# Second net of a three-stage kernel put under the planner that orders the first two stages

## The chip, the core and the metric

One core of one Trainium2 chip runs the whole program. The metric is the device time of one execution in microseconds. Three runs of the kernel before took 1053.13, 1054.54 and 1055.58 us (median 1054.54). The execution that was profiled took 1055.07 us, of which the trace spans 1053.2 us from the first to the last instruction. Engines are named as in the profile: PE (TensorE, with PEld for its weight loads), DVE (VectorE), ACT (ScalarE), POOL (GpSimd) and SP (SyncE, which here only issues DMAs).

## The reference, cut to what matters

```python
# 1. retention: q, k, v of 4 batches, 8 heads, 768 positions, 64 features
state = gamma * state + einsum('bhd,bhe->bhde', k[:, :, t], v[:, :, t])
y[:, :, t] = scale * einsum('bhd,bhde->bhe', q[:, :, t], state)
x = y as (3072 tokens, 512)
# 2. first net: w_in (512, 2048), w_out (2048, 512)
h = x @ w_in
g = where(h >= 1, h, where(h <= -1, 0, (h + 1)**2 / 4))
x = g @ w_out
# 3. second net: w1, w2 (512, 1024), w3 (1024, 1024), w_out (1024, 512)
out = ((x @ w1) * (x @ w2)) @ w3 @ w_out
```

All arrays are float32.

## The kernel before

**Arithmetic.** Every product of the two nets is made of three matmuls of 128x128 by 128x512 in the type fp32r: an operand is split into a high half (ACT casts it to fp32r) and a low half (DVE subtracts the high half from the source), and high·high, low·high and high·low are summed in one PSUM bank. So nearly each operand costs one ACT and one DVE instruction, a "split", before PE can use it.

**The second net.** Its two last weights are multiplied first: 16 units of 12 matmuls (8 for each half of w3) give w3·w_out in four PSUM banks a half, and each bank is split into a tile `wc`. Units read w3's rows from DRAM, where an earlier stage left them (`w3f`), and split them (`w3s`). The 6 token tiles are then taken as 3 pairs. For a pair, 14 operands (`yop`) are split from the first net's output and its sums and differences; for each of 8 blocks f of 128 hidden features a weight "unit" is loaded (`unit_w`), split, summed and split again, and 7 products p1, p2, p6, p5, p7, p3, p4 of 6 matmuls each go to the banks a, c and b. This gives both tiles' a and b by 7 products where 8 would be needed directly. ACT and DVE join them to the two gated products `c`, which are split into `p` and `q`. The products of `p` with `wc` (L984, banks `oacc`) stand between the products of the next block; those of `q` follow at the pair's end, 24 matmuls for each of 4 token groups t. `oacc` has 4 banks; each finished bank is copied out (`ost`, on DVE for even t, on ACT for odd t) and stored.

**What sets the order.** Stages 1 and 2 are recorded as operations of a planner (class `Plan`): each has an engine, a cost, the values it reads and writes, and slots of named pools ("tags") that its values need. `set_due` walks back from PE's list, which is written out by hand, and gives each operation a due time; `emit` then issues, at every step, the operation that could start first, among those of an engine the one due soonest, and PE may take any ready one of its next 12. What `emit` issues on an engine stays in that order on the chip: each engine runs its own list in order and waits at an instruction until its semaphores are there. The second net is not in that plan: it is emitted after `plan.emit` (L1174) by the loops of L1195 to L1254, in the order in which they are written. There `load_w3(u + 1)` stands ahead of `emit_w3o(u)` (L1196, L1197), the unit's sums are GpSimd's (L904), and at a pair's end the next pair's splits are written between the blocks and the copies of `oacc`:

```python
            for x in out_blocks(NF2 - 2):
                emit_out(*x)
            if more:
                while ahead[0][1] == 0:
                    split_y(*ahead.pop(0))
                fetch_y1(i + 1, 1, range(4))
            for x in out_blocks(NF2 - 1):
                emit_out(*x)
                evac_out(2 * i, x[3], x[0])
```

The tiles of w3's split halves come from a pool of two on the right side of SBUF (`late[1]`, tag "ws", L862), made once the weight conversion's pool is closed (L1176). The first net's operands `g` and `wo` use a pool of ten slots, tag "wo" (L285). A weight that arrives as 64-bit words is converted by `convert` (two ACT and four DVE instructions a KB row); seven of w3's eight row blocks are converted before and spilled to DRAM, one (`DIRECT`) at the end of the first net.

## Time and profile before

| | us |
|---|---|
| median of 3 runs | 1054.54 (1053.13 to 1055.58) |
| the profiled execution | 1055.07 |
| its span in the trace | 1053.2 |
| from the first to the last start of PE in the second net | 618.26 to 1048.94 |

The first two stages fill the span up to about 617 us, w3·w_out runs to 668 us, and the three pairs follow at 668, 799 and 928 us or so. A timeline row gives the start and the duration in us; an idle time in brackets stands ahead of the row's first instruction, with the engine and line that ended it. Matmul durations overlap (they are pipelined), so the pace of PE is read from start to start.

### The profile page before, as it was taken

Reading aid. Unit: us, or ns where it says so; the run is one execution under the profiler, and the core shown is the slowest. Engines: PE = TensorE matmul, PEld = TensorE weight load, DVE = VectorE, ACT = ScalarE, POOL = GpSimd, SP = SyncE. Lnnn points to the kernel's source line nnn. Section 1 sums busy time; section 2 is a strip of 40 time slices with the busy share of each in tenths; the row PEclk is TensorE's granted clock in tenths of the full one; section 3 lists DMA queues with packets and bytes.
Section 4 is the critical chain, followed back from the end, with each engine's and each line's share of the span. In section 5 each row is a group of like instructions: output and inputs, shape, how many; then the busy total and the mean of one; then the engine's idle time right before and its main releaser. Section 6 shows DMA issues by size and latency. Waiting matters only on the chain.

```text
span 1053.2 us, 14552 instructions
## 1 busy us (share of the span) xinstructions
PE 1020.0 (97%) x5444; PEld 824.1 (78%) x5444; DVE 644.6 (61%) x957; ACT 500.8 (48%) x845; POOL 165.5 (16%) x221
## 2 busy tenths in 40 slices
PE   8899999999999999999999989899989999899998
PEld 5778878877877788888887868688867888678886
DVE  6887479734465684777776657465573556635550
ACT  2477457533344552566666535444442444334330
POOL 1212332222232100000000000222211322022210
PEclk8999999999999999999999999899999999899999
DMA  9997959757979689781453963112122120221102
GB/s 291 239 308 239 317 182 407 286 193 275 372 256 381 201 309 338 262 295 65 180 179 101 347 231 101 40 41 84 37 90 91 40 80 21 101 80 41 40 1 80
DMA packets 71051, 190.18 MB, mean 181 GB/s; under 512 B 8898, under 2 KB 9282, under 8 KB 69060
## 3 DMA queue, kind: packets, MB, share of 16 engines
q1 hardware_dynamic: 63104, 163.34, 45.7%
q0 software_dynamic: 7584, 25.70, 6.3%
q8 instruction: 43, 0.70, 0.3%
q14 instruction: 28, 0.23, 0.1%
q10 hardware_dynamic: 292, 0.20, 0.1%
HBM read 139.40 MB, written 49.81 MB: 180 GB/s over the span
## 4 chain that ended last, share of the span: by engine, by line
PE 85%; DMA 6%; ACT 3%; DVE 2%; SPq 1%; issue 1%; POOL 0%; DVEq 0%; POOLq 0%; ACTq 0%
PE bank_a L946 12%; PE y1acc L277 8%; PE y1acc L279 8%; PE y1acc L278 8%; PE bank_b L946 6%; PE hps L277 5%; PE hps L279 5%; PE hps L278 5%; PE oacc L987 4%; PE oacc L989 4%; PE oacc L988 4%; PE bank L731 4%; PE banks L731 3%; PE bank_c L946 3%; DMA raw<-in_w_in_dram 3%; PE pa L530 1%
## 5 line engine op out<-in xcount | busy, mean ns | idle before, releaser
L904 POOL TENSOR_TENSOR unit_w<-unit_w 128x256 f32<-128x256 f32 x96 | 70.9, 738 | 576.4 <-DVE unit L274 570.8
L277 PE MATMUL y1acc<-g,wo 128*128 128x512 f32 x384 | 151.7, 395 | 2.4 <-DMA wo<-wo_d 1.3
L946 PE MATMUL bank_a<-yop,unit 128*128 128x512 f32 x576 | 147.6, 393 | 6.3 <-ACT c L961 4.3
L279 PE MATMUL y1acc<-g,wo 128*128 128x512 f32 x384 | 149.8, 390 | 0.0
L278 PE MATMUL y1acc<-g,wo 128*128 128x512 f32 x384 | 149.6, 390 | 0.0
L946 PEld LDWEIGHTS bank_a<-yop,unit 128*128 128x128 f32 x576 | 108.4, 189 | 30.2 <-ACT c L961 4.7
L277 PE MATMUL hps<-xh,win 128*128 128x512 f32 x256 | 102.9, 402 | 2.9 <-ACT xh L573 1.8
L279 PE MATMUL hps<-xl,win 128*128 128x512 f32 x256 | 100.6, 393 | 0.0
L278 PE MATMUL hps<-xh,win 128*128 128x512 f32 x256 | 100.6, 393 | 0.0
L277 PEld LDWEIGHTS y1acc<-g,wo 128*128 128x128 f32 x384 | 72.1, 188 | 20.8 <-ACT r L613 1.7
L973 DVE TENSOR_TENSOR c<-bank_b,c 128x512 f32<-128x512 f32 x24 | 16.6, 692 | 115.6 <-PE bank_b L946 115.6
L613 ACT ACTIVATE r<-hps 128x512 f32<-128x512 f32 x64 | 38.2, 597 | 98.8 <-PE hps L279 97.3
L279 PEld LDWEIGHTS y1acc<-g,wo 128*128 128x128 f32 x384 | 72.1, 188 | 15.5 <-DVE g L338 0.4
L278 PEld LDWEIGHTS y1acc<-g,wo 128*128 128x128 f32 x384 | 72.1, 188 | 14.5
L336 ACT CAST g<-g 128x512 fp32r<-128x512 f32 x80 | 48.9, 620 | 68.1 <-PE y1acc L279 59.0
L616 DVE SCALAR_TENSOR_TENSOR r<-hps,r 128x512 f32<-128x512 f32 x64 | 44.0, 688 | 53.5 <-ACT r L615 52.9
L946 PE MATMUL bank_b<-yop,unit 128*128 128x512 f32 x288 | 74.0, 393 | 0.0
L338 DVE TENSOR_TENSOR g<-g 128x512 fp32r<-128x512 f32 x64 | 44.8, 713 | 32.9 <-ACT g L336 32.8
L946 PEld LDWEIGHTS bank_b<-yop,unit 128*128 128x128 f32 x288 | 54.8, 190 | 11.7
L274 DVE TENSOR_TENSOR unit<-unit_w,unit 128x512 fp32r<-128x512 f32 x96 | 57.2, 617 | 8.2 <-ACT unit L273 8.2
L277 PEld LDWEIGHTS hps<-xh,win 128*128 128x128 f32 x256 | 48.6, 190 | 16.8 <-DVE r L616 3.0
L621 POOL DMA_DIRECT2D g_d<-r x64 | 37.3, 583 | 138.1 <-DVE r L616 130.2
(186 smaller groups left out, 1935.8 us busy)
## 6 DMA issues: line engine op xcount, KB each, us to landing
wo<-wo_d SPq DMA_DIRECT2D x64, 512.0 KB, 5.5
g_d<-r POOLq DMA_DIRECT2D x64, 256.0 KB, 5.0
g<-g_d SPq DMA_DIRECT2D x64, 256.0 KB, 5.3
unit_w<-sp_wab SPq DMA_DIRECT2D x24, 512.0 KB, 3.5
wo_d<-wo POOLq DMA_DIRECT2D x16, 512.0 KB, 7.3
raw<-in_w_dram SPq DMA_DIRECT2D x16, 512.0 KB, 6.8
raw<-in_w3t_dram SPq DMA_DIRECT2D x8, 1024.0 KB, 7.6
raw<-in_w_in_dram SPq DMA_DIRECT2D x28, 256.0 KB, 7.9
```

Source lines behind the costliest of these rows:

```text
L274: nc.vector.tensor_tensor(out=lo, in0=src, in1=hi, op=ALU.subtract)
L277: nc.tensor.matmul(out=ps, lhsT=lh, rhs=rh, start=first, stop=False)
L278: nc.tensor.matmul(out=ps, lhsT=ll, rhs=rh, start=False, stop=False)
L279: nc.tensor.matmul(out=ps, lhsT=lh, rhs=rl, start=False, stop=last)
L336: plan.op("ACT", 0.63, lambda: nc.scalar.copy(out=dst.ap[:, 0, :], in_=at()), r=[src], w=[dst, hi], bound=bound)
L338: return plan.op("DVE", 0.7, lambda: nc.vector.tensor_tensor(out=dst.ap[:, 1, :], in0=at(), in1=dst.ap[:, 0, :], op=ALU.subtract), r=[src, ...
L616: plan.op("DVE", 0.7, lambda: nc.vector.scalar_tensor_tensor(out=r.ap, in0=ps.ap, scalar=1.0, in1=r.ap, op0=ALU.max, op1=ALU.min), r=[ps], ...
L731: nc.tensor.matmul(out=at[where](), lhsT=l, rhs=r, start=first and kb + k == 0, stop=kb == 1 and k == 2, skip_group_check=True,)
L904: nc.gpsimd.tensor_tensor(out=block(u, o), in0=block(u, x), in1=block(u, y), op=op)
L946: nc.tensor.matmul(out=ps, lhsT=x, rhs=z, start=first and kb + k == 0, stop=kb == 1 and k == 2, skip_group_check=True,)
L987: nc.tensor.matmul(out=ps, lhsT=lh, rhs=wh, start=(f == 0), stop=False)
L988: nc.tensor.matmul(out=ps, lhsT=lh, rhs=wl, start=False, stop=False)
```

## The change

The second net's operations are recorded with `plan.op` too, before the one call of `emit`; their PE operations are appended to PE's list by hand, in nearly the order that the loops had, and the planner chooses where ACT, DVE, SP put theirs. The unit's sums become DVE operations, because the second net now uses the first net's `plan_unit`. The split halves of w3 take slots of the tag "wo". Stores are marked `store`: they are due 6 us after what they store, and are not counted among the loads that hold SP's window of 30 us. `DIRECT` falls to 0 and `FEW` rises to 4, so that all eight blocks of w3 are spilled, and the last conversions are due 14 us ahead instead of 4. Two pools are closed and others opened by operations of the plan (`close_conversion`, and `close_pairs`, whose banks b and c then take). The tag "y" has 6 slots (4 before).

```diff
-DIRECT = 1
-FEW = 3
+DIRECT = 0
+FEW = 4
...
                     last = min((a.due for a in o.after), default=self.FAR)
+                    if o.store:
+                        last = min(last, max(d.due + d.cost for d in o.deps) + 6.0)
...
-        loads = {o for o in self.ops if o.eng == "SP"}
+        loads = {o for o in self.ops if o.eng == "SP" and not o.store}
...
-    def load_w3(u):
-        if u < 2 * NF2:
-            t = late[1].tile([P, 2, 512], F32R, tag="ws", name="w3s", bufs=2)
-            split(t[:, 0, :], t[:, 1, :], arrived.pop(("w3", u)))
-            w3[u] = t
...
-        for o, x, y, op in SUMS:
-            nc.gpsimd.tensor_tensor(out=block(u, o), in0=block(u, x), in1=block(u, y), op=op)
...
+    def plan_w3o(u):
+        hf, j = divmod(u, NF2)
         if j == 0:
+            banks["w3", hf] = y_banks(None, False)
+        src, i, got = w3.pop(u)
+        t = Val("wo", lambda: new_wo("w3s"))
+        plan_split(t, src, (slice(None), i), got=got)
...
+        w3_ops[u] = plan.op("PE", 2.724, fn, r=[t, t2], w=[v for v, _ in banks["w3", hf]])
+        if j == NF2 - 1:
+            for m, (v, _) in enumerate(banks["w3", hf]):
+                w = wc[4 * hf + m] = Val("g5", lambda: late[0].tile([P, 2, 512], F32R, tag="wc", name="wc", bufs=NF2))
+                plan_split(w, v, (slice(None),))
+
+    def plan_ab_unit(n):
+        src, stored = spill["wab", n % NF2]
+        return plan_unit(Val("w", lambda: wpool.tile([P, 1024], F32, tag="w", name="unit_w")), src, [], [stored])
...
+        for u in range(2 * NF2):
+            plan_w3o(u)
+            pe.append(w3_ops[u])
+        for i in range(NTILE // 2):
+            for kb in range(2):
+                plan_pair_y(i, kb)
+            for f in range(NF2):
+                plan_ab(i, f)
+                for t in range(4):
+                    plan_out(i, 0, f, t)
...
+            for f in range(NF2):
+                a, b = ab_ops[i, f], blocks_of(f - 1) if 0 < f < NF2 - 1 else [None] * 4
+                pe += [o for o in (a[0], a[1], b[0], a[2], a[3], b[1], a[4], a[5], b[2], a[6], b[3]) if o]
+            pe += blocks_of(NF2 - 2) + blocks_of(NF2 - 1)
+            for t in range(4):
+                pe += [out_ops[i, 1, f, t] for f in range(NF2)]
```

PE's matmuls and DMA volumes stay as they are but for w3's converted block (stored and read back). Three places show what the plan makes of it; line numbers are those of each kernel's own file.

On ACT, from the end of the first net into w3's units, before (`y1st` copies out the first net's last banks, `w3s` is w3's high half, `yop` a pair operand, `g` the first net's operand, `wo` the second net's w_out):

```order
L336 CAST wo_5553<-u 128x512
L310 ACTIVATE u<-raw 128x1024
L313 ACTIVATE raw<-raw 128x1024
L832 COPY y1st<-y1acc 128x512 x2
L273 CAST w3s<-w3f 128x512 x5
L273 CAST yop<-f_5615 128x512
```

and the same place now:

```order
L337 CAST g<-g_5242 128x512
L337 CAST w3s<-w3f 128x512 x2
L337 CAST wo_5571<-u 128x512
L337 CAST wo_5574<-u 128x512
L337 CAST w3s<-w3f 128x512 x6
L656 CAST unit<-unit_w 128x512
L656 CAST unit<-unit_w 128x256
L337 CAST w3s<-w3f 128x512
L834 COPY y1st<-y1acc 128x512 x2
L337 CAST w3s<-w3f 128x512
```

Nine of w3's splits stand ahead of the two copies, and the first unit's first casts too; before, all of them stood behind.

On PE, where w3's halves meet the first block, before:

```order
L277 MATMUL w3acc<-wo_5547,w3s 128x512
L278 MATMUL w3acc<-wo_5547,w3s 128x512
L279 MATMUL w3acc<-wo_5547,w3s 128x512
L946 MATMUL bank_a<-yop,unit 128x512 x6
L946 MATMUL bank_c<-yop,unit 128x512 x6
L946 MATMUL bank_a<-yop,unit 128x512 x6
```

and now, at the end of w3's first half (`y1acc` here is the name of w3's banks):

```order
L276 MATMUL y1acc<-wo_5574,w3s 128x512
L277 MATMUL y1acc<-wo_5574,w3s 128x512
L278 MATMUL y1acc<-wo_5574,w3s 128x512
L934 MATMUL bank_a<-yop,unit 128x512 x6
L934 MATMUL bank_c<-yop,unit 128x512 x6
L276 MATMUL y1acc<-wo_5273,w3s 128x512
L277 MATMUL y1acc<-wo_5273,w3s 128x512
L278 MATMUL y1acc<-wo_5273,w3s 128x512
```

The first block's p1 and p2 moved from behind the second half to between the halves. Elsewhere in the second net PE's order is the same.

On DVE at the first pair's end, before (`p` and `q` are the low halves of the gated products, `t_` the differences for the next pair):

```order
L274 TENSOR_TENSOR q<-c_6642,q 128x512
L923 TENSOR_TENSOR t__6716<-f_6538,f_6536 128x512
L924 TENSOR_TENSOR t__6717<-f_6542,f_6538 128x512
L925 TENSOR_TENSOR t__6716<-f_6542,t__6716 128x512
L926 TENSOR_TENSOR t__6717<-f_6540,t__6716 128x512
L274 TENSOR_TENSOR yop<-f_6536,yop 128x512
L274 TENSOR_TENSOR yop<-f_6540,yop 128x512
L274 TENSOR_TENSOR yop<-t__6716,yop 128x512 x2
L274 TENSOR_TENSOR yop<-t__6717,yop 128x512
L274 TENSOR_TENSOR yop<-f_6542,yop 128x512
L274 TENSOR_TENSOR yop<-t__6717,yop 128x512
L834 COPY ost<-oacc 128x512 x2
```

and now:

```order
L339 TENSOR_TENSOR p<-c,p 128x512
L339 TENSOR_TENSOR p<-c_6602,p 128x512
L339 TENSOR_TENSOR p<-c_6694,p 128x512
L836 COPY ost<-oacc 128x512
L664 TENSOR_TENSOR unit_w<-unit_w 128x256
L836 COPY ost<-oacc 128x512
L664 TENSOR_TENSOR unit_w<-unit_w 128x256
L899 TENSOR_TENSOR t__6711<-y,t__6711 128x512
L916 TENSOR_TENSOR yop<-y,yop 128x512
L658 TENSOR_TENSOR unit<-unit_w,unit 128x512 x2
```

The copies of `oacc` stand directly behind the last splits of `p`, ahead of the next pair's operands, and single sums of a unit stand between them. On ACT the casts of the next pair's operands move behind its two copies in the same way.

## Rows read from the trace of the kernel before

**Rows 1.** The page, part 1: busy us of each engine, share, instructions.
```profile
PE 1020.0 (97%) x5444; PEld 824.1 (78%) x5444; DVE 644.6 (61%) x957; ACT 500.8 (48%) x845; POOL 165.5 (16%) x221
```

**Rows 2.** Stretches: length, busy us (instructions) by engine, granted PE clock, DMA share, GB/s.
```profile
903.00:908.00 5.00, 5.00 (x12) 3.94 (x13) 4.61 (x8) 1.46 (x3) 0.00 (x0) 0.50 0.70 250
778.00:783.00 5.00, 5.00 (x24) 4.12 (x23) 4.67 (x8) 1.48 (x3) 0.00 (x0) 1.00 0.70 250
625.60:628.80 3.20, 3.20 (x9) 2.50 (x8) 0.00 (x0) 0.00 (x0) 0.00 (x0) 0.50 1.05 399
100.00:617.00 517.00, 513.26 (x2958) 415.44 (x2956) 339.81 (x484) 274.68 (x444) 72.88 (x93) 1.00 0.71 257
618.00:1050.00 432.00, 415.82 (x1776) 336.89 (x1776) 225.46 (x367) 169.07 (x318) 70.86 (x96) 0.98 0.21 69
```

**Rows 3.** Waits of PE, whole span: total us, times, longest us.
```profile
PE oacc L987 <- ACT ost L832: 6.1, 2, 3.1
...
PE bank_a L946 <- ACT c L966: 2.0, 2, 1.0
...
PE y1acc L277 <- DMA wo<-wo_d: 1.3, 1, 1.3
...
PE y1acc L277 <- ACT y1st L832: 0.9, 1, 0.9
...
PE banks L731 <- DVE c L764: 0.2, 1, 0.2
```

**Rows 4.** Timeline of PE: end of the first net and w3's units.
```profile
610.10 0.39 PE L277 MATMUL y1acc<-g,wo 128*128 128x512 f32 x1
...
616.68 0.39 PE L279 MATMUL y1acc<-g,wo 128*128 128x512 f32 x1
618.26 0.49 PE L277 MATMUL w3acc<-wo,w3s 128*128 128x512 f32 x1 [1.19 <-ACT w3s L273]
...
624.22 0.50 PE L277 MATMUL w3acc<-wo,w3s 128*128 128x512 f32 x1 [2.40 <-ACT w3s L273]
...
629.16 0.39 PE L277 MATMUL w3acc<-wo,w3s 128*128 128x512 f32 x1
...
668.28 0.39 PE L279 MATMUL w3acc<-wo,w3s 128*128 128x512 f32 x1
```

**Rows 5.** Timeline of ACT: the last first-net copy, then the first block.
```profile
617.10 0.59 ACT L832 COPY y1st<-y1acc 128x512 f32<-128x512 f32 x1 [0.77 <-PE y1acc L279]
...
671.54 1.14 ACT L273 CAST unit<-unit_w 128x512 fp32r<-128x512 f32 x2 [4.18 <-POOL unit_w L904]
```

**Rows 6.** Timeline of PE: the first block after w3's units.
```profile
669.88 1.52 PE L946 MATMUL bank_c<-yop,unit 128*128 128x512 f32 x6
675.68 2.92 PE L946 MATMUL bank_a<-yop,unit 128*128 128x512 f32 x6 [4.28 <-ACT c L961]
...
680.61 1.52 PE L946 MATMUL bank_a<-yop,unit 128*128 128x512 f32 x6
```

**Rows 7.** Timeline of PE: the ends of the first and second pair.
```profile
773.98 0.39 PE L989 MATMUL oacc<-wc,p 128*128 128x512 f32 x1
777.42 0.50 PE L987 MATMUL oacc<-wc,q 128*128 128x512 f32 x1 [3.06 <-ACT ost L832]
...
899.44 0.39 PE L989 MATMUL oacc<-wc,p 128*128 128x512 f32 x1
902.89 0.80 PE L987 MATMUL oacc<-wc,q 128*128 128x512 f32 x1 [3.06 <-ACT ost L832]
...
908.60 0.52 PE L988 MATMUL oacc<-wc,q 128*128 128x512 f32 x1
```

**Rows 8.** Timeline of ACT: the first pair's end.
```profile
776.80 1.06 ACT L832 COPY ost<-oacc 128x512 f32<-128x512 f32 x2
```

**Rows 9.** Groups by line and shape: count, busy us, mean ns, idle before.
```profile
L973 DVE TENSOR_TENSOR c<-bank_b,c 128x512 f32<-128x512 f32 x24 | 16.6, 692 | 115.6 <-PE bank_b L946 115.6
L664 DVE TENSOR_TENSOR u<-u 128x256 f32<-128x256 f32 x32 | 13.5, 423 | 0.9
```

More of the change, by code (lines that the diff above doesn't have):

```diff
@@ L867, in emit_w3o, with load_w3 @@
+    def load_w3(pair):
+        t = Val("g5", lambda: late[0].tile([P, 2, 512], F32, tag="wc", name="w3f", bufs=NF2))
+        for i, u in enumerate(pair):
+            src, stored = spill["w3", u]
+            got = Val(None, None)
+            plan.op("SP", 0.43, lambda i=i, src=src: nc.sync.dma_start(out=t.ap[:, i, :], in_=src),
+                    part=[t, got], size=256, after=[stored])
+            w3[u] = t, i, [got]
+    def plan_w3o(u):
         hf, j = divmod(u, NF2)
         if j == 0:
-            accs[hf] = [psum["acc"].tile([P, 512], F32, tag="acc", name="w3acc") for _ in range(4)]
@@ new lines, in plan_out, with fn @@
+    def plan_out(i, n, f, t):
+        p, w = pq[i, f, n], wc[f]
+        if f == 0:
+            evacs[i, n, t] = Val("acc", lambda: psum["acc"].tile([P, DM], F32, tag="acc", name="oacc"))
+        ps = evacs[i, n, t]
+        def fn():
+            lh, ll = (p.ap[:, s, t * P:(t + 1) * P] for s in range(2))
+            wh, wl = w.ap[:, 0, :], w.ap[:, 1, :]
+            nc.tensor.matmul(out=ps.ap, lhsT=lh, rhs=wh, start=(f == 0), stop=False)
+            nc.tensor.matmul(out=ps.ap, lhsT=lh, rhs=wl, start=False, stop=False)
+            nc.tensor.matmul(out=ps.ap, lhsT=ll, rhs=wh, start=False, stop=(f == NF2 - 1))
+        out_ops[i, n, f, t] = plan.op("PE", 0.681, fn, r=[p, w], w=[ps])
+        if f < NF2 - 1:
+            return
+        st = Val("st", lambda: new_st("ost"))
+        r0 = t * S + (2 * i + n) * C
+        parts = [(t % 2, nc.sync, 0, 512)]
+        if 2 * i + n == NTILE - 1 and t == 3:
+            parts = [(0, nc.sync, 0, 256), (1, nc.scalar, 256, 512)]
+        for eng, queue, c0, c1 in parts:
+            done = Val(None, None)
+            plan.op("ACT" if eng else "DVE", 0.63, lambda eng=eng, c0=c0, c1=c1: evacuate(
+                st.ap[:, c0:c1], ps.ap[:, c0:c1], eng), r=[ps], part=[st, done])
+            plan.op("ACT" if queue is nc.scalar else "SP", 0.43, lambda queue=queue, c0=c0, c1=c1: queue.dma_start(
+                out=out[r0:r0 + P, c0:c1], in_=st.ap[:, c0:c1]), r=[done], use=[st], size=(c1 - c0) / 2).store = True
@@ new lines, in close_conversion, with close_pairs @@
+        def close_conversion():
+            conversion.close()
+            late.append(ctx.enter_context(tc.tile_pool(name="later", bufs=1, side="right")))
+        def close_pairs():
+            pairs_psum.close()
+            psum["b"] = ctx.enter_context(tc.tile_pool(name="ps_b", bufs=1, space=bass.MemoryType.PSUM))
+        users = lambda *tags: [o for o in plan.ops if any(x.tag in tags for x in o.vals)]
+        converted = plan.op("POOL", 0.0, close_conversion, after=[*users("raw", "u"), closed])
```

355 lines of the change are left out of this document (122 added, 233 removed), and 1 row of the table plan.

## The prediction

> **What bounds the kernel now.** Read the page's first part: PE is busy 97% of the span, DVE 61%, ACT 48% [rows 1]. So a gain can only come from PE's idle or slow time, and the next question is where that lies. The stretches answer it. From 100 to 617 us, where the planner orders everything, PE idles 517 − 513.3 = 3.7 us and is granted the full clock. From 618 to 1050 us, in the second net, it idles 432 − 415.8 = 16.2 us at a mean clock of 0.98 [rows 2]. Third, PE's waits: the large ones of the second net are for ACT, each once or twice [rows 3, 4, 6]. None of them repeats in the 24 blocks, where DVE waits for PE instead: 115.6 us in all ahead of the join with bank b [rows 9]. So the second net is bound by PE within its blocks and by the order of ACT's and DVE's lists where its stages meet. PE's work is unchanged, so the sum is that of these meetings.
>
> The pace to measure them against: from 610.10 to 616.68 us 29 matmuls start, 0.227 us each [rows 4].
>
> **w3's start.** From 616.68 to 629.16 us 25 matmuls start [rows 4]; at 0.227 that is 5.7 us, it took 12.5, so 6.8 us are lost: 1.35 ahead of the first w3 matmul (618.26 − 616.68 − 0.23), 2.4 and some 1.0 in single waits for the splits, the rest at a lower clock. Before, ACT's splits of w3 stand behind its two copies of the first net's banks. Now eight of them stand ahead in slots of "wo" that the first net gives back block by block, two slots of ten a block; PE reaches the units with their operands made. That takes away all but the first wait. The first I keep: the ninth split also stands ahead of the two copies on ACT, the ten slots are then taken by eight splits and the last first-net block, so it waits for that block's end. In the trace that lets ACT start at 617.10; one cast (two take 1.14) and one copy (0.59) later it is 618.26 [rows 5], and the first w3 group needs the bank of ACT's first copy. So PE starts when it did before. Gain 6.8 − 1.35 = 5.45 us. DVE's two copies could hold w3 up too: they now stand behind a difference of freshly loaded `y` tiles. The bounds are a load that comes late as once in the first net, 1.3 us [rows 3], and the first wait gone as well: 4.15 to 6.8 us.
>
> Between 625.6 and 628.8 the granted clock was 0.50, the lower level of 1.2 GHz, right behind two waits; it was 1.00 behind the 3.06 us wait at 777 and 0.50 again behind an equal one at 903 [rows 2, 7]. So a wait may or may not be followed by a slow stretch. The Trainium skill (TensorE: Matmul & The Clock Gate, Part 1) says that the half-rate clock is the default and that only recent activity holds it off. By that rule the 1.35 us that stays is short beside full work and costs nothing more; if it were nevertheless followed by a slow stretch as at 625 us, the sum would be about 1.6 us worse. The trace agrees that PE's earlier work matters, since equal waits of 3.06 us end either way; no row shows one wait of 1.35 us by itself.
>
> **w3's pace.** From 629.16 to 668.28 us 167 matmuls start in 39.12 us: 0.2343 each [rows 4], 0.0075 more than the first net's. In the code what sets them apart is the stationary tile: `w3s` in the right-hand pool, where the first net's `wo` and all others of that pace lie in pools on the left. Now `w3s` lies in slots of "wo". I take the whole difference, 167 x 0.0075 = 1.2 us; the other end is 0.
>
> **The first block.** From 669.88 to 680.61 us 18 matmuls start, 4.1 us at the full pace; 6.6 us are lost [rows 6], 4.28 of them waiting for ACT's copy c1. ACT was behind GpSimd's sums by 4.18 us [rows 5]. Now p1 and p2 stand between w3's halves, with 8 units, 22 us, for the copy and the joins before p6 wants the bank; the sums are DVE's in that time. Their operands need the pair's tiles and DVE's list: some 21 DVE instructions of 0.69 stand there between 618 and 640, 15 us of 22. p6 and p5 then run beside the second half's four evacuations on ACT, of which two can run before p6 ends, so c2's copy finds ACT free. Gain 6.6; the lower end is half, if the last operand for p1 or p2 is late by 3 us.
>
> **The pair's ends.** At 773.98 and 899.44 us PE waits for `ost`, 3.06 us each [rows 7]. The bank's last matmul was long done: ACT's copies stood behind casts of the next pair's operands and began at 776.80 [rows 8]. Now DVE's copy of the first bank stands right behind the last `p` split, and ACT's two ahead of the operands. The last block's first bank is done 9 matmuls, 2.0 us, before the block's end, and DVE needs 0.7 us: no wait. Gain 777.42 − 773.98 − 0.23 = 3.2 us, and for the second end 908.60 − 899.44 − 14 x 0.227 = 6.0 us, slow clock included [rows 7]. Behind both ends PE waited once more in the next first block, 1.0 us each [rows 3], where ACT stood behind a late weight unit; the unit's load now stands ahead of the output stores on SP. Gain 2.0. What is late next: the yops of the next pair, with 24 us of PE work ahead of their use.
>
> **DVE's new work.** 96 sums of 128x256 at 0.423 us [rows 9] add 41 us to DVE, which is busy 225 of 432 us there [rows 2]: 62% after. Block by block: ten instructions of 0.69 and one of 0.42 for joins and splits, four sums: 9.0 us, against 42 matmuls or 9.5 us of PE at f = 0 and 7 and 54, 12.3 us, between. They fit, and the unit is made one block ahead, so they cost nothing; were that cover gone they cost 1.7 us a block.
>
> **Other edits.** The eighth spilled block of w3 adds a store and a load at a DMA share of 0.21 later and 0.71 earlier [rows 2], and one conversion in the first net in place of the one at its end: nothing. The due times of stores shift a few instructions in the first two stages. There the planner left PE waits of 1.3, 0.9 and 0.2 us [rows 3]. I take 0, with ±2.5.
>
> **The sum.** Gains 5.45 + 1.2 + 6.6 + 3.2 + 6.0 + 2.0 = 24.5 us. New small waits: at the rate of the planner's own stretch, 2.4 us in 517, the second net gets 2.0 in 432; 1.35 of it is counted already, so 0.7. From the profiled execution: 1055.07 − 24.5 + 0.7 = 1031.3 us. It lies 0.5 above the median, so 1030.8, and I say 1031 us.
>
> **Rivals.** *The waits move.* Each list is now ordered by planned durations, and an early-placed split that waits for a slot or a load holds everything behind it, as the ninth split does. If w3's start loses the 5.45 again, or the first block its 6.6, the time is 1036 to 1038; both, 1043. For it: the lists are tight just there, with DVE's copies behind a load. Against: planned the same way, 517 us show only 3.7 us idle.
>
> *DVE becomes the bound.* If DVE's list runs behind, each unit's sums stand ahead of the join that frees a bank, and all 96 are on the path: +41 − 24.5, about 1047 to 1071. It decides from 12.3 − 9.0 = 3.3 us more DVE time a block. Against: 115.6 us of DVE waiting for PE. This is the slower side, from about 1.1 us a block on.
>
> *The first net pays.* A load of w_out or a conversion late by one wait of each kind: +2.4, with a slow stretch of 2.8 as at 903 us: 1036.
>
> *The change hardly acts*, because PE's list is the old one and slots gate the splits: if only the pair's ends are mended, 1055 − 11 = 1043.
>
> **How the numbers follow.** The forecast, 1028 to 1034: 0.66. Waits that move, 1034 to 1043: 0.16. The first net, 1034 to 1037: 0.07. Hardly acts, 1040 to 1046: 0.06. DVE bound: 0.05, of which one half ends within 0.2% or slower. A difference of 0.2%, 2 us, is what can just be told from no change. So faster 0.95, same 0.015, slower 0.035. The lower end is all of PE's 16.2 us and its slow time gone, and the first net 2 better: 1027. The range 1027 to 1040 leaves out some 2 in 10.
>
> **What the profile will show.** Right: the first w3 matmul some 1.3 us behind the last first-net one with ACT's `y1st` named, and none at the second unit; w3's matmuls 0.227 apart; p1 and p2 near 640 us with no idle time, p6 at once behind the second half; `q` matmuls directly behind `p`'s; DVE some 265 us busy from 618 us on; idle PE time there below 4 us. Wrong: waits for `w3s`, `yop` or `unit` in PE's list, a clock of 0.50 anywhere after 100 us, w3's matmuls still 0.234 apart, or PE's idle time before 617 us up by more than 2.5.

## The result, and the profile after

The changed kernel takes 1027.4 us (median of 4 runs, 1024.02 to 1029.22) against 1055.06 us before on the same chip (4 runs, 1053.13 to 1056.87): a ratio of 0.973, interval 0.970 to 0.977. The execution that was profiled took 1026.57 us, 4.7 below the 1031.3 that the sum gave for a profiled execution.

The page's first part and the stretches, to be read beside [rows 1, 2], come first; the second net now runs from 618 to 1020 us.

```profile
PE 1004.5 (98%) x5444; PEld 819.0 (80%) x5444; DVE 691.0 (67%) x1053; ACT 503.1 (49%) x845; POOL 96.0 (9%) x125
```

```profile
100.00:617.00 517.00, 514.37 (x2978) 417.35 (x2976) 346.25 (x495) 279.13 (x455) 74.64 (x94) 1.00 0.74 267
618.00:1020.00 402.00, 401.72 (x1772) 332.66 (x1773) 265.93 (x454) 168.90 (x308) 0.00 (x0) 1.00 0.19 64
```

PE idles 0.3 us of 402 where it idled 16.2 of 432, and the clock is the full one in both stretches. DVE's busy time went from 225 to 266 us, as the sums ask.

Before 617 us PE is busy 514.4 us, before the change 513.3. The first net's last start is at 616.70 where it was at 616.68, but two differences of 2.0 us cancel in that. Its 101st matmul (counted over `hps`, the product with `w_in`) starts 2.0 us later than before, and from there to its last start it takes 549.73 us instead of 551.72. Two rows of the kernel before and one of the changed kernel:

```profile
64.96 0.39 PE L278 MATMUL hps<-xh,win 128*128 128x512 f32 x1
...
260.40 0.47 PE L277 MATMUL y1acc<-g,wo 128*128 128x512 f32 x1 [1.30 <-DMA wo<-wo_d]
```

```profile
66.97 0.39 PE L277 MATMUL hps<-xh,win 128*128 128x512 f32 x1
```

PE's waits over the whole span are these, against [rows 3]:

```profile
PE rows_ps L1012 <- DMA rows<-in_c_decay_dram: 2.6, 1, 2.6
...
PE y1acc L276 <- ACT y1st L834: 1.7, 2, 1.2
```

The first row lies in the first 100 us. The last one holds the one wait left in the second net, 1.19 us at its first matmul. PE no longer waits for copies of `oacc` or `bank_a`.

PE's timeline at w3 (against [rows 4, 6]; `y1acc` beside `w3s` is the name of w3's banks now):

```profile
616.70 0.39 PE L278 MATMUL y1acc<-g,wo 128*128 128x512 f32 x1
618.28 0.50 PE L276 MATMUL y1acc<-wo,w3s 128*128 128x512 f32 x1 [1.19 <-ACT y1st L834]
...
623.85 0.39 PE L276 MATMUL y1acc<-wo,w3s 128*128 128x512 f32 x1
...
640.17 1.52 PE L934 MATMUL bank_a<-yop,unit 128*128 128x512 f32 x6
...
664.43 0.39 PE L278 MATMUL y1acc<-wo,w3s 128*128 128x512 f32 x1
664.65 0.62 PE L934 MATMUL bank_a<-yop,unit 128*128 128x512 f32 x2
...
1020.75 0.39 PE L983 MATMUL oacc<-wc,p 128*128 128x512 f32 x1
```

The row at 623.85 is w3's 25th matmul: 24 starts in 5.57 us. From there to 664.43 stand 179 starts (12 are p1's and p2's) in 40.58 us, 0.2267 each. p6 follows at 664.65 with no gap. From 618.28 to 1020.75, 1775 starts take 402.47 us: 0.2267 each, with 0.13 us lost.

ACT at w3's start (against [rows 5]):

```profile
617.12 0.62 ACT L337 CAST w3s<-w3f 128x512 fp32r<-128x512 f32 x1 [0.70 <-PE y1acc L278]
617.65 1.07 ACT L834 COPY y1st<-y1acc 128x512 f32<-128x512 f32 x2
618.60 0.63 ACT L337 CAST w3s<-w3f 128x512 fp32r<-128x512 f32 x1
```

This is the ninth split ahead of the two copies, as the prediction read it from the order.

At w3's second unit PE waited 2.40 us in the kernel before [rows 4]. The rows of SP and ACT from that trace show what ACT's split was waiting for there, a load of w3 that SP issues behind the first net's last stores (SPq are SP's DMA issues, `y_d` the stores, `w3f` the loads):

```profile
617.24 1.78 SPq L839 DMA_DIRECT2D y_d<-y1st  x4
619.11 2.20 SPq L857 DMA_DIRECT2D w3f<-sp_w  x4
```

```profile
623.55 1.31 ACT L273 CAST w3s<-w3f 128x512 fp32r<-128x512 f32 x2 [5.35 <-DMA w3f<-sp_w]
```

In the changed kernel the first of these loads is issued 46 us earlier, and ten stand ahead of the first net's end:

```profile
573.25 0.38 SPq L856 DMA_DIRECT2D w3f<-sp_w  x1
```

At the first pair's end ACT's casts of the next pair's operands stood directly ahead of the copies in the kernel before; this row is followed by that of [rows 8]:

```profile
776.28 0.61 ACT L273 CAST yop<-t__6717 128x512 fp32r<-128x512 f32 x1
```

DVE at the same place now:

```profile
755.99 1.90 DVE L339 TENSOR_TENSOR p<-c,p 128x512 fp32r<-128x512 f32 x3
758.01 0.69 DVE L836 COPY ost<-oacc 128x512 f32<-128x512 f32 x1
```

### A measure for all runs

The times of single runs of one kernel spread by 4 to 5 us. Much of that arises at the start: in the 18 profiles the first net's 101st matmul starts between 64.0 and 68.6 us. So the runs are compared by what PE loses in a stretch: the time between the starts of two matmuls, less 0.22667 us for each matmul between. (In the best profile below, 1775 starts of the second net take 402.34 us, which is 0.22667 each.) "First w3 wait" runs from the first net's last start to w3's first, "rest of w3" to w3's last, and "`p` to `q`" from a pair's first `p` matmul to its first `q` matmul. In us:

| kernel | first w3 wait | next 24 | rest of w3 | to first `p` of pair 1 | pair 1, `p` to `q` | to pair 2's `p` | pair 2 | to pair 3's `p` | pair 3 |
|---|---|---|---|---|---|---|---|---|---|
| before | 1.35 | 5.46 | 1.27 | 6.77 | 4.22 | 1.57 | 4.22 | 4.29 | 0.54 |
| after | 1.35 | 0.13 | 0.01 | 0 | 0 | 0 | 0 | 0 | 0 |
| `oacc` copies first | 1.35 | 5.55 | 1.28 | 6.33 | 1.00 | 1.33 | 0.97 | 1.67 | 0.53 |
| sums on DVE | 1.35 | 5.82 | 1.27 | 3.25 | 4.18 | 3.14 | 4.18 | 3.35 | 0.54 |
| `p` first | 1.35 | 5.30 | 1.28 | 6.19 | 5.77 | 2.86 | 5.77 | 3.57 | 1.45 |
| unit load first | 1.36 | 5.40 | 1.27 | 6.33 | 4.21 | 0.26 | 4.20 | 1.85 | 0.49 |
| five edits by hand | 1.35 | 5.68 | 0.03 | 4.61 | 1.45 | 0 | 1.45 | 0 | 1.45 |
| four edits by hand | 1.35 | 6.87 | 0.46 | 4.95 | 0.97 | 0.11 | 0.97 | 0.12 | 0.48 |

Behind the first wait the kernel before loses 28.35 us and the changed one 0.14: a gain of 28.2 where the sum had 23.8.

### The profile page after: what moved, and what is told of

It is laid out like the page before. It is cut to its first block, busy times and chain, and to the rows that moved or that the text cites. A ratio compares the mean times of both kernels' runs of the same rounds, so it can differ in the third digit from the quotient of the medians.

```text
span 1024.8 us, 14489 instructions
## 1 busy us (share of the span) xinstructions
PE 1004.5 (98%) x5444; PEld 819.0 (80%) x5444; DVE 691.0 (67%) x1053; ACT 503.1 (49%) x845; POOL 96.0 (9%) x125
## 4 chain that ended last, share of the span: by engine, by line
PE 93%; DMA 3%; DVE 1%; ACT 1%; issue 1%; SPq 0%; ACTq 0%; DVEq 0%
PE bank_a L934 13%; PE y1acc L276 10%; PE y1acc L277 10%; PE y1acc L278 10%; PE bank_b L934 6%; PE hps L276 6%; PE hps L278 5%; PE hps L277 5%; PE oacc L982 4%; PE oacc L981 4%; PE oacc L983 4%; PE bank L733 4%; PE banks L733 3%; PE bank_c L934 3%; DMA raw<-in_w_in_dram 2%; PE pa L532 2%
## 5 line engine op out<-in xcount | busy, mean ns | idle before, releaser
L942 ACT COPY c<-bank_a 128x512 f32<-128x512 f32 x72 | 42.3, 587 | 98.0 <-PE bank_a L934 95.7
L658 DVE TENSOR_TENSOR unit<-unit_w,unit 128x512 fp32r<-128x512 f32 x96 | 59.0, 622 | 28.3 <-ACT unit L656 27.9
L981 PE MATMUL oacc<-wc,p 128*128 128x512 f32 x192 | 74.7, 389 | 0.0
L982 PE MATMUL oacc<-wc,p 128*128 128x512 f32 x192 | 74.7, 389 | 0.0
L983 PE MATMUL oacc<-wc,p 128*128 128x512 f32 x192 | 74.7, 389 | 0.0
L656 ACT CAST unit<-unit_w 128x512 fp32r<-128x512 f32 x96 | 53.6, 568 | 28.4 <-PE bank_b L934 14.6
L934 PEld LDWEIGHTS bank_b<-yop,unit 128*128 128x128 f32 x288 | 54.1, 188 | 11.2
```

Source lines behind the costliest of these rows:

```text
L656: plan.op("ACT", 0.18 + 0.00088 * (b - a), lambda: nc.scalar.copy(out=hi(), in_=u.ap[:, a:b]), r=[u], part=[v, done])
L658: plan.op("DVE", 0.15 + 0.00106 * (b - a), lambda: nc.vector.tensor_tensor(out=lo(), in0=u.ap[:, a:b], in1=hi(), op=ALU.subtract), r=[u, d ...
L934: nc.tensor.matmul(out=vals[where].ap, lhsT=l, rhs=r, start=first and kb + k == 0, stop=kb == 1 and k == 2, skip_group_check=True,)
L981: nc.tensor.matmul(out=ps.ap, lhsT=lh, rhs=wh, start=(f == 0), stop=False)
L982: nc.tensor.matmul(out=ps.ap, lhsT=lh, rhs=wl, start=False, stop=False)
L983: nc.tensor.matmul(out=ps.ap, lhsT=ll, rhs=wh, start=False, stop=(f == NF2 - 1))
```

## The experiments

### The changed kernel with one part undone

**The first block's p1 held behind w3**, then **the whole old order of p1, p2, p6, p5**:

```diff
+        w3_ops[2 * NF2 - 1].after.append(ab_ops[0, 0][0])
+        ab_ops[0, 0][0].deps.add(w3_ops[2 * NF2 - 1])
```

> The changed kernel, with the first block's p1 and p2 held behind w3's second half, where they stood in the kernel before; the rest planned as in the changed kernel. Theory A (the first block's 6.6 us were lost because p1 and p2 stood there): PE waits again ahead of p6 for ACT's copy of the bank, some 3 to 6 us, time 1030 to 1033. Theory B (they were lost because ACT's list had a GpSimd-fed cast ahead of that copy, and the planner puts the copy first now): at most 0.5 to 2 us come back, time 1027.5 to 1029.5.

```diff
+        line = [w3_ops[2 * NF2 - 1]] + ab_ops[0, 0][:4]
+        for x, y in zip(line, line[1:]):
+            x.after.append(y)
+            y.deps.add(x)
```

> The changed kernel, with PE's order of the first block as in the kernel before: p1, p2, p6, p5 one behind the other, all behind w3's second half (with p1 alone held back, p2 stayed between the halves and p5 went ahead of p6, and nothing was lost). Theory A (the place of p1 and p2 is what pays the first block's 6.6 us): PE waits ahead of p6 for ACT's copy of the bank, 3 us or more, second net 405.5 us or more from its first w3 start to its last start. Theory B (ACT's list is what pays: c1's copy stands ahead of the casts of w3's banks and of the unit): under 0.5 us, second net 402.5 to 403.

Measured: ratio to before 0.973 (0.971 to 0.975) for both; 402.47 and 402.46 us in the second net, where the changed kernel has 402.47. That is theory B, without even the small loss that the first run allowed. These are PE and ACT in the second of them:

```profile
659.66 0.39 PE L278 MATMUL y1acc<-wo,w3s 128*128 128x512 f32 x1
659.89 1.52 PE L934 MATMUL bank_a<-yop,unit 128*128 128x512 f32 x6
661.25 1.52 PE L934 MATMUL bank_c<-yop,unit 128*128 128x512 f32 x6
662.61 1.52 PE L934 MATMUL bank_a<-yop,unit 128*128 128x512 f32 x6
```

```profile
625.94 1.14 ACT L656 CAST unit<-unit_w 128x512 fp32r<-128x512 f32 x2 [4.56 <-DVE unit_w L664]
...
661.45 0.59 ACT L942 COPY c<-bank_a 128x512 f32<-128x512 f32 x1 [2.13 <-PE bank_a L934]
661.93 1.08 ACT L337 CAST wc<-y1acc 128x512 fp32r<-128x512 f32 x2
```

PE's order is that of before, but c1's copy starts 0.2 us after p2's first matmul and stands ahead of two of the four casts of `wc`. It takes 0.59 us, while PE spends 1.36 on p2. So the swap paid nothing; ACT's list paid the 6.6 us.

Two things differ in that list, and the rows show both. One is the place of the copy among the casts of `wc`. The other is the first unit: ACT waits for its sums here too, 4.56 us, but 34 us ahead of the copy. In the kernel before this unit's load was issued some 50 us later (its row, then this run's), so its last casts stood between p1 and the copy [rows 5]:

```profile
654.66 0.32 SPq L893 DMA_DIRECT2D unit_w<-sp_wab  x1
```

```profile
601.85 0.42 SPq L652 DMA_DIRECT2D unit_w<-sp_wab  x1
```

p6 reads the first of those casts, which are made from the sums, and it began at 671.54, half a microsecond behind the start of p2's last matmul. So the copy's place alone could not have paid all of the loss. No run moves the copy without the unit or the unit without the copy.

**The sums back on GpSimd:**

```diff
+            eng, cost, e = ("POOL", 0.75, nc.gpsimd) if u.tag == "w" else ("DVE", 0.43, nc.vector)
+            plan.op(eng, cost, lambda o=o, x=x, y=y, op=op, e=e: e.tensor_tensor(
...
```

> The changed kernel with the second net's unit sums put back on GpSimd, which the planner is told costs 0.75 us each. Theory (with a list ordered by due times the sums' engine costs nothing, since the units are made a block ahead): second net within 1 us of the changed kernel's 402.5 us from the first w3 start to the last start, time 1026 to 1029. Rival (GpSimd's hand-over is what held ACT up in the first block, whoever orders the lists): 3 to 5 us lost again near w3's end or in the first blocks.

Measured 0.972 (0.970 to 0.975), second net 402.47 us. Once the lists are ordered by due times, it doesn't matter which engine makes the sums.

**w3's splits no more than two units ahead:**

```diff
+        first = len(plan.ops)
         plan_split(t, src, (slice(None), i), got=got)
+        if u > 1:
+            plan.ops[first].deps.add(w3_ops[u - 2])
+            w3_ops[u - 2].after.append(plan.ops[first])
```

> The changed kernel, with one rule more: the split of w3's unit u may not be issued before PE's unit u - 2 stands, so that no more than two slots' worth of splits is made early. Theory (the first w3 wait is left over because the ninth early split waits for a slot of wo and holds ACT's two copies of the first net's last banks): ACT copies earlier, PE's first w3 start comes 0.2 to 0.6 us behind the first net's last instead of 1.58, the rest of w3 keeps its pace; 1.0 to 1.3 us less than the changed kernel. Rival 1 (the copy waits for PE's last matmul anyway, and PE for the copy): the wait keeps at least 0.9 of its 1.19 us. Rival 2 (the early splits are needed): waits for w3s come back behind the first unit, 2 to 5 us more.

```profile
615.98 0.39 PE L278 MATMUL y1acc<-g,wo 128*128 128x512 f32 x1
616.20 0.39 PE L276 MATMUL y1acc<-wo,w3s 128*128 128x512 f32 x1
...
1018.54 0.39 PE L987 MATMUL oacc<-wc,p 128*128 128x512 f32 x1
```

The first wait is gone entirely. ACT's first `y1st` copy started at 615.04, before the first net's last matmul, and 402.56 us pass from that matmul (615.98) to the last start where the changed kernel needs 404.05. That is 1.5 us less, the size of the wait. In time it is 1025.4 us, ratio 0.9715 (0.9693 to 0.9737): the best version here, though times alone can't tell it from the changed kernel. The theory holds, a little above its 1.0 to 1.3 us: two splits ahead are enough, and the ninth one made the wait.

### The kernel before with one part done

**The `oacc` copies ahead of the next pair's splits:**

```diff
-            if more:
-                add_y(i + 1, 0)
             for x in out_blocks(NF2 - 2):
                 emit_out(*x)
-            if more:
-                while ahead[0][1] == 0:
-                    split_y(*ahead.pop(0))
-                fetch_y1(i + 1, 1, range(4))
             for x in out_blocks(NF2 - 1):
                 emit_out(*x)
                 evac_out(2 * i, x[3], x[0])
             if more:
+                add_y(i + 1, 0)
+                while ahead[0][1] == 0:
+                    split_y(*ahead.pop(0))
+                fetch_y1(i + 1, 1, range(4))
...
```

> The kernel before, with only the order at a pair's end changed as the planner has it: the copies of oacc are written ahead of the next pair's sums and splits. Theory (each pair end is lost by ACT's list alone, and the predicted 3.2 and 6.0 us are its price): both waits of 3.06 us go, with the slow clock behind the second, and the time falls by 9.2 us, to about 1045.5; the two further waits of 1.0 us in the next first block stay, since the weight unit's load keeps its place behind the stores. Rival 1 (the wait moves): the operands of the next pair are now late, and PE waits for yop in the next block; gain 3 to 6 us. Rival 2 (it is the late unit that goes too): gain 11 us.

Measured 0.994 (0.992 to 0.996), 1047.9 us. In the table the pair ends fall from 4.22 to 1.00 and 0.97, and the slow stretch behind the second goes as well: 9.7 us less in the second net, 0.5 above the theory (in time it is 7.7). These are ACT there, and PE, which now goes on without a wait:

```profile
773.57 0.59 ACT L832 COPY ost<-oacc 128x512 f32<-128x512 f32 x1 [1.49 <-PE oacc L989]
774.99 0.59 ACT L832 COPY ost<-oacc 128x512 f32<-128x512 f32 x1 [0.83 <-PE oacc L989]
775.48 0.62 ACT L273 CAST yop<-f 128x512 fp32r<-128x512 f32 x1
```

```profile
774.74 0.39 PE L987 MATMUL oacc<-wc,q 128*128 128x512 f32 x1
```

The 1.0 us that stays in each pair's `p` to `q` is no listed wait. It is a term that the prediction did not have, and the next experiment but one looks at it.

**The sums on DVE:**

```diff
-            nc.gpsimd.tensor_tensor(out=block(u, o), in0=block(u, x), in1=block(u, y), op=op)
+            nc.vector.tensor_tensor(out=block(u, o), in0=block(u, x), in1=block(u, y), op=op)
```

> The kernel before, with only the unit's 96 sums moved from GpSimd to VectorE, in the old written order. Theory (in the first block ACT's c1 stood behind the cast of a unit that waited 4.18 us for GpSimd): that wait shrinks to the duration of four sums of 0.42 us and the first block loses about 4 us less; elsewhere the unit is made a block ahead and the sums cost nothing; time 4 to 5 us lower. Rival 1 (ACT would wait for the bank anyway): no change, within 1 us. Rival 2 (DVE becomes the bound, the sums stand ahead of joins that free banks): slower by up to 41 us, PE waits for DVE's c in every block.

Measured 0.998 (0.997 to 1.000). The first block's loss falls from 6.77 to 3.25; ahead of pair 2 it grows to 3.14, where this run has a slow stretch behind the first pair's end (below). In all it is 2.6 us less, not the 4 to 5 of the theory. These are ACT's row that was [rows 5]'s second, and the copy that PE waits for:

```profile
670.33 1.14 ACT L273 CAST unit<-unit_w 128x512 fp32r<-128x512 f32 x2 [2.71 <-DVE unit_w L904]
671.38 2.04 ACT L273 CAST wc<-w3acc 128x512 fp32r<-128x512 f32 x4
673.29 0.65 ACT L273 CAST yop<-t__5836 128x512 fp32r<-128x512 f32 x1
673.81 0.62 ACT L961 COPY c<-bank_a 128x512 f32<-128x512 f32 x1
```

ACT still waits 2.71 us for the sums, only from a faster engine. What keeps c1's copy is everything that stands ahead of it: that wait and seven casts. A faster sum mends part of it. The planned list, in which neither that wait nor the unit's casts stand between p1 and the copy, mends all of it.

**`p` ahead of a unit's last splits** (the step calls between and behind p4 are left to the loop's end):

```diff
...
-        between()
+        between(False)
         product("p4", bank, False)
         nc.vector.tensor_tensor(out=c1, in0=bank, in1=c1, op=ALU.mult)
-        between()
+        between(False)
```

> The kernel before, with a unit's two last splits written behind the block's splits of p and q, where they stood ahead of the join with bank a and ahead of p. Theory (the 17 gaps of 0.10 to 0.16 us among the p matmuls of the blocks f = 1 and 7, 2.1 us in all, come from p's halves that DVE makes just too late, since it does a unit's split first): they go, 2.1 us less in the second net. Rival (they come from the hand-over from ACT or DVE to PE, whatever stands ahead): they stay. Against both: units that are now late for the next block's p1, up to 1 us a block.

Measured 1.004 (1.002 to 1.006): slower. The theory's gaps do go, all 17, but three new waits for c1 come and the two at the pairs' ends grow:

```profile
PE oacc L988 <- ACT ost L832: 8.3, 2, 4.2
PE bank_a L946 <- ACT c L962: 6.4, 4, 4.2
```

The unit's casts, moved behind `p`, now stand ahead of the next block's c1 copy, and 1.0 us of them ahead of the pair's last copies. So the gaps did come from DVE's unit splits ahead of `p`, and moving these by hand costs more than it saves.

**The second unit's load ahead of the stores:**

```diff
-                if 0 < n < n_units - 1:
+                if 0 < n < n_units - 1 and f:
                     load_unit(n + 1)
...
+                load_unit(NF2 * (i + 1) + 1)
             for x in out_blocks(NF2 - 1):
```

> The kernel before, with one load moved: at a pair's end the second unit of the next pair is loaded ahead of the stores of the output, where it stood behind all eight. Theory (the two waits for ACT's c2 in the first blocks of the second and third pair, 1.18 and 1.13 us with small ones of 0.13 behind them, come from that load, which keeps ACT waiting at the unit's cast): both go, 2.6 us less. Rival (ACT is late there for its copy of the last output): they stay.

Measured 0.997 (0.995 to 0.999). Ahead of pair 2 the loss falls from 1.57 to 0.26 and ahead of pair 3 from 4.29 to 1.85; no wait for c2 is left. The second figure has a slow stretch in it, shorter in this run (mean granted clock 0.72 over the 6 us behind the wait, 0.50 before). The load is the cause of the waits for c2.

**All five edits together, then without the moved unit splits:**

> The kernel before with the single edits put together and still without a planner in the second net: the copies of oacc ahead of the next pair's splits, the sums on VectorE, w3's halves in wo's slots, p ahead of a unit's last splits, and the second unit's load ahead of the stores. Theory (the change's gain is a sum of separate meetings): the gains add, 9.7 + 2.6 + 1.3 + 2.1 + 2.6 = 18.3 us, so the second net takes 412.4 us from its first w3 start to its last start and the time is about 1037; what is left to the changed kernel's 402.5 is w3's start and the rest of the first block. Rival (one list of an engine is shared by all, so the edits collide): at least 4 us of the 18.3 missing.

Measured 0.987 (0.984 to 0.989), 1040.7 us; 417.0 us in the second net where 412.4 was forecast. The rival holds, 4.6 us are missing. They show at two places: 1.45 in each pair, where the moved splits make a wait for c1 of 0.71 us, and 4.61 in the first block, where the sums alone had left 3.25.

> The kernel put together by hand as before but without the moved splits of the unit, which by themselves had made the kernel slower. Theory (that edit alone collided, the other four add): losses of 5.5 at w3's start, 0 in the rest of w3, 3.3 in the first block, 1.0 at each pair's end and 0.5 in the third pair, under 0.5 ahead of the second and third pair: some 12 us in all, so 414 to 414.6 us from the first w3 start to the last start, time about 1038. Rival (VectorE's sums collide with the copies of oacc at the pairs' ends): 416 us or more.

Measured 0.988 (0.985 to 0.992), 1043.8 us; 417.3 us in the second net, where the theory had 414 to 414.6 and the rival 416 or more. The pairs come out as the theory says to 0.2 us (0.97, 0.11, 0.97, 0.12, 0.48), so the rival's collision isn't there, though its number is met. What misses is ahead of them: 6.87 at w3's start, where ACT waited 6.11 us for the load of w3 after 5.35 in the kernel before, 0.46 in the rest of w3 and 4.95 in the first block, where waits still stood; from 668 to 690 us the granted clock was 0.92. The profile is of one of three runs that took 1043.7 to 1044.1 us; the fourth took 1036.7. So the edits add in the pairs, while what a wait that is left in costs beside itself moved by 1 to 2 us from profile to profile.

### What sets w3's pace

The tiles' places are read from the built programs: before, each `w3s` starts 96 bytes behind a multiple of 128, `wo` and all other tiles of the two nets' 128x512 matmuls on a multiple. Six runs move them, four in the kernel before and two in the changed kernel, nearly all by a small tile that shifts a pool:

```diff
         load_w3(0)
+        pad = late[1].tile([P, 8], F32, tag="pad", name="pad")
+        nc.gpsimd.memset(pad, 0.0)
```

> The kernel before, with 32 more bytes a partition in the pool of w3s, so that w3's split halves, the stationary tiles of w3's matmuls, move from byte 32 of a 64-byte line to byte 0, where all other stationary tiles of this kernel lie. Order and everything else as before. Theory (the offset in the line sets the pace): from the second w3 unit's 629 us to the end of w3's units the matmuls start 0.227 us apart where they started 0.2343 apart, 1.2 us in 167 matmuls, and the time falls by about 1.2 us. Rival (the pool of two or the side of SBUF sets it, or slots that are refilled just in time): 0.234 stays, time within 0.5 us of before.

The same with 24 columns:

> The kernel before, with 96 more bytes in the pool of w3s, so that w3's split halves start at a multiple of 128 bytes, as every other stationary tile of the kernel does; with 32 bytes more they started at an odd multiple of 64, and the pace only went from 0.2343 to 0.2334. Theory (the alignment sets the pace, and 128 bytes is the step): 0.227 from start to start in w3's second half. Rival (what sets it is the pool: its place at the end of SBUF, or its two slots): 0.233 to 0.234.

In the slots of `wo`, in the old order:

```diff
-            t = late[1].tile([P, 2, 512], F32R, tag="ws", name="w3s", bufs=2)
+            t = new_wo("w3s")
```

> The kernel before in its old written order, with w3's split halves in the ten slots of wo instead of a pool of two. Theory on the pace (pool or place): 0.227 in w3's second half, 1.2 us less in all. Theory on the start (it is the order on ACT, not the lack of slots, that makes PE wait at the second unit): the single wait of 2.4 us there stays within 0.5 us. Together about 1.2 to 2 us less than before. Rival (slots alone mend the start): the wait at the second unit goes, 5 to 6 us less.

All pools of the changed kernel shifted:

```diff
+    shift = ctx.enter_context(tc.tile_pool(name="shift", bufs=1)).tile([P, 8], F32, tag="shift", name="shift")
+    nc.gpsimd.memset(shift, 0.0)
     wpool = ctx.enter_context(tc.tile_pool(name="wpool", bufs=16))
```

> The changed kernel, with every tile of the weight, operand and gated-product pools 32 bytes further on, so that all stationary (and moving) tiles of the two nets start 32 bytes behind a multiple of 128 where they started on it. Theory (w3's pace in the kernel before was set by the offset of its tiles: 0.2343 at 96 bytes, 0.2333 at 64, 0.2267 at 0): all matmuls of 128x512 go to 0.233 to 0.2343 from start to start; over 1776 of the second net that is 12 to 14 us, and about as much again or more over the 2,280 or so between 100 and 617 us, so 25 to 35 us slower, about 1055. Rival (only w3's tiles in their place at the end of SBUF feel it): within 2 us of the changed kernel.

The pad with 16 columns, in the kernel before, and then the shift of all pools with 24, in the changed kernel:

> The kernel before, with 64 more bytes in the pool of w3s, so that w3's split halves (stationary) start 32 bytes behind a multiple of 128, while w_out's (moving) still start on one. Measured so far: 0.2343 from start to start with the stationary tile at 96 and the moving one at 0, 0.2333 at 64 and 0, 0.2267 at 0 and 0, and 0.2267 with both at 32. Theory A (the difference of the two offsets counts): 0.233 to 0.2345, 1.1 to 1.3 us lost in 167 matmuls. Theory B (the stationary tile's own offset counts, and 32 is harmless): 0.2267, no loss.

> The changed kernel, with every tile of the two nets' pools 96 bytes further on, stationary and moving ones alike. Theory A (the difference of the two offsets counts): 0.2267 everywhere, second net 402.5 us from its first w3 start to its last start. Theory B (the stationary tile's own offset counts, and 96 is a bad one): 0.234 to 0.235, second net 13 us longer and the whole kernel 25 to 35 us slower.

These are PE's rows of w3's 25th and last matmul, 167 starts apart, with `w3s` at 64, at 0, in `wo`'s slots, and at 32:

```profile
628.36 0.39 PE L277 MATMUL w3acc<-wo,w3s 128*128 128x512 f32 x1
...
667.32 0.40 PE L279 MATMUL w3acc<-wo,w3s 128*128 128x512 f32 x1
```

```profile
632.28 0.39 PE L277 MATMUL w3acc<-wo,w3s 128*128 128x512 f32 x1
...
670.13 0.39 PE L279 MATMUL w3acc<-wo,w3s 128*128 128x512 f32 x1
```

```profile
628.67 0.39 PE L277 MATMUL w3acc<-wo,w3s 128*128 128x512 f32 x1
...
666.52 0.39 PE L279 MATMUL w3acc<-wo,w3s 128*128 128x512 f32 x1
```

```profile
628.84 0.40 PE L277 MATMUL w3acc<-wo,w3s 128*128 128x512 f32 x1
...
667.81 0.40 PE L279 MATMUL w3acc<-wo,w3s 128*128 128x512 f32 x1
```

| stationary `w3s`, moving `wo`: bytes behind a multiple of 128 | us a start |
|---|---|
| 96, 0 (before) | 0.2343 |
| 64, 0 | 0.2333 |
| 32, 0 | 0.2333 |
| 0, 0 (two places) | 0.2267 |
| 32, 32 | 0.2267 |
| 96, 96 | 0.2267 |

With all tiles at 32 or 96 the second net takes 402.47 and 402.46 us. So 128 bytes is the step, the place in SBUF and the number of slots don't matter, and neither does a tile's own offset: what costs is that the two operands' offsets differ. The way there had misses. At 64 a start took 0.2333 us, where the theory had 0.227 and the rival had 0.234 staying; and with all tiles at 32 the theory asked for 25 to 35 us more, and nothing came. That left two theories, whose forecasts for the last two runs differ, and both runs came out as theory A. The wait at the second unit stayed in `wo`'s slots (3.0 us there, 0.6 more than before where 0.5 was allowed), so slots alone don't mend w3's start. The theory put it down to ACT's order, but ACT's row there is idle for 5.96 us until a load of w3 lands. In time these edits of about 1 us drown: 1.000 (0.999 to 1.002) for the first, 1.000 (0.998 to 1.002) in `wo`'s slots, and single runs of 1057.2 (at 0), 1054.5 (at 32), 1024.8 and 1024.6 us.

## Where the prediction was wrong, and what of it held

The change gained more than the prediction's range allows. The measured ratio of 0.9734, taken of the 1054.54 us that the prediction started from, is 1026.5 us, below the range's lower end of 1027 and well below the 1028 to 1034 that had 0.66. The median of 1027.4 stands beside a kernel before at 1055.06. It isn't one odd result: three variants whose second net takes the same 402.47 us (one without the first block's swap, one with the old order, one with the sums on GpSimd) had medians of 1025.6 to 1026.3 us, beside 1054.8 to 1055.6 for the kernel before.

The step that failed is the one that took the second net's loss as the sum of its named waits, with nothing lost inside the blocks. What the runs showed in its place: the second net lost 28.35 us behind its first wait, and 28.2 of them came back, where the sum had 23.8. The missing part lies at the pairs, 14.84 us where 11.2 were counted: gaps of 0.10 to 0.16 us among `p`'s matmuls, with what goes with them 2.55 us, and waits for c2 of 3.1 us instead of 2.0. The lower end had the same fault: with 2 us for the first net it left some 26 us for the second (1055 − 1027 − 2).

The rest of the mechanism held: PE's work is the bound, and the planner took away what was lost where stages meet. At w3's second unit the prediction also named the wrong list, without harm to its sum. Step by step:

- **w3's start.** The table has 6.81 before (1.35 and 5.46, forecast 6.8) and 1.48 after (forecast 1.35), with `y1st` named in PE's row and the cause of this wait shown by the run that lets the splits start two units ahead. The wait at the second unit went as forecast, but not for the reason given. The prediction had ACT's splits stand behind its two copies, and gained by slots of "wo". That holds for the first unit; at the second ACT sat idle for 5.35 us until a load of w3 landed, which SP had issued at 619.11, behind the first net's last stores. What the plan changed there is SP's list: its loads start at 573.25. Slots alone did not mend it, and with only two splits ahead nothing was lost. So the right number of this step, 5.33 us gained for 5.45, is in part luck. No run moves those loads alone. The wait that stays was not followed by a slow stretch: the next 24 starts lose 0.13 us at a granted clock of 1.00. By the clock rule that the prediction cited (the Trainium skill, TensorE: Matmul & The Clock Gate, Part 1) it should cost nothing more, and this trace agrees to 0.13 us.
- **w3's pace.** 1.27 gained, forecast 1.2. The reason given (the pool, its place) was half right: the move to `wo`'s slots mends it, because it makes the offsets of the two operands equal.
- **The first block.** 6.77 gained, forecast 6.6. The step's first reason fell: moving p1 and p2 is not needed. Its row of ACT behind GpSimd [rows 5] was a part; the whole is ACT's list, with a first unit made more than 40 us earlier and c1's copy ahead of the last casts of `wc`. How much each of the two pays is open.
- **The pair ends.** Here the sum was short. 3.2 + 6.0 + 2.0 = 11.2 were counted; the table's last five columns hold 14.84. Two terms make the 3.6: c2's waits, with the small ones behind them, are 3.1 and not 2.0 (1.57 ahead of pair 2; 4.29 less the slow stretch of 2.8 ahead of pair 3). And 2.55 us are lost among `p`'s matmuls, 1.0 in each of the first two pairs and 0.54 in the third, most of it as 17 gaps of 0.10 to 0.16 us where DVE makes `p` just too late. No view of waits shown here lists such gaps, and the prediction took its terms from waits.
- **New small waits.** 0.7 were added for those that a planner leaves; 0.14 came.
- **DVE.** 41 us more of sums cost nothing (266 busy of 402), and GpSimd's would not have either.
- **Other edits.** 0 was taken for the first two stages, with ±2.5. From the 101st matmul on they gained 2.0 us in this pair of profiles. The seven profiles with the changed plan take 549.73 to 549.79 us there, the eleven of the old one 550.23 to 551.72. What undid it here, the later start, differs from profile to profile in both kernels (64.0 to 68.6 us). Which edit brought the gain is open: the stores' due times, `DIRECT`, `FEW` and the slots of "y" were not undone one by one. The outputs' tail gave 0.2.

So 4.4 of the 4.7 us between sum and measurement are these: 3.6 at the pairs, 0.6 of waits that did not come (0.7 less the 0.13 lost behind the first wait), 0.2 in the first block and the pace. A count of the starts would have said it: 1775 starts at the pace of the first net, 0.2267, are 402.4 us, and the kernel before took 430.7, so 28.3 were to be had; the prediction named 24.5 of them and put its lower end at PE's idle and slow time gone, without working that out as starts times pace.

None of the rivals came: no wait moved, the first net paid nothing, DVE did not become the bound, and far more than the pair's ends was mended.

## What to carry to other kernels

Bound a stretch by starts times the best pace that the trace shows before adding up its waits; what the waits don't explain lies in gaps too short to be listed. Where an engine waits for a copy, look at what stands ahead of that copy in its own list: clearing that list, with the first unit made early, paid all of the first block here, a faster engine for the work ahead paid half, and reordering PE's products nothing. And follow a late split back to its load: at w3's second unit the split was late because SP issued the load behind stores. An edit of one list by hand moves waits on others, as the run that put `p` first shows; so measure each such edit alone and in company.

## What the runs showed of the hardware that was not expected

A 128x512 matmul of this type starts every 0.2267 us when its stationary and its moving tile lie equally far behind a multiple of 128 bytes in SBUF, and every 0.2333 to 0.2343 us when they don't (differences of 32, 64 and 96 bytes): 3% of PE's pace. This is shown for w3's matmuls; a moving tile shifted alone was not tried.

Two equal waits are not followed by the same clock. These are the 6 us behind each pair's end (granted clock third from the right), in the kernel before and in the run with the sums on DVE:

```profile
777.42:783.42 6.00, 6.00 (x26) 4.99 (x27) 5.67 (x10) 2.48 (x5) 0.00 (x0) 1.00 0.74 270
902.89:908.89 6.00, 6.00 (x14) 4.74 (x15) 5.58 (x10) 2.38 (x5) 0.00 (x0) 0.50 0.75 270
```

```profile
774.13:780.13 6.00, 6.00 (x19) 4.84 (x20) 5.59 (x10) 2.40 (x5) 0.00 (x0) 0.72 0.78 269
901.13:907.13 6.00, 6.00 (x19) 4.81 (x20) 5.45 (x10) 2.25 (x5) 0.00 (x0) 0.72 0.71 266
```

Of eight profiles that kept both waits, the second is followed by the lower level of 1.2 GHz for part or all of the stretch in all eight (mean 0.50 to 0.72), the first in three. What decides it is open. The prediction read in the equal waits that PE's earlier work matters; they show only that a wait's length alone does not decide. The clock's two levels there are why the table's columns "to pair 2's `p`" and "to pair 3's `p`" differ, by 2.7 us in the kernel before and by 1.6 with the unit load first, where the order is the same.
